# Last stage of a fused H3 and gated-MLP backward pass: partner spectra by a lane shuffle, halo rows by a shifted-identity matmul, merged weight-gradient stores, and a new order

## The chip, the cores and the metric

One core of one Trainium2 chip. The metric is device time in microseconds of one execution; a kernel's time is the median of several executions. The core has the engines TensorE (PE, with its weight loads PEld), VectorE (DVE), ScalarE (ACT), GpSimd (POOL) and SyncE (SP), and 16 DMA engines that all DMA queues share. In this kernel SP issues nearly all DMAs, and ACT issues some.

## The reference, cut to what matters

The reference computes the output of a block and, through `jax.vjp`, the gradients of nine inputs, for one sequence of S = 2048 tokens, D = 512 channels and F = 1376 hidden channels, in bf16:

```python
k_shift = sum over t of k_pad[:, t:t+S] * shift_k[:, 3-t]      # 4 taps per channel
kv = k_shift * v
y  = irfft(rfft(kv padded to 2S) * rfft(ssm_k padded to 2S))[:S] + kv * ssm_D
s  = xn * y                                                    # xn = layernorm(x)
h  = sigmoid(xn @ w_gate) * (xn @ w_up)
out = x + s * silu(h @ w_down)
# returned: out, and the gradients of x (A_q), k, v, shift_k, ssm_k, ssm_D, w_gate, w_up, w_down
```

The last stage, which the change edits, makes two groups of gradients. The weight gradients are products over all tokens: `d w_down = h^T dz` (1376 x 512) and `d w_gate`, `d w_up = xn^T dg`, `xn^T du` (512 x 1376 each). The gradients of k, v, shift_k, ssm_k and ssm_D go back through the long convolution: the spectrum of the incoming gradient is multiplied by the stored spectra of the kernel and of kv, and both products are transformed back.

## The kernel before, in words

Everything lives in one SBUF slab and one PSUM tile of 8 banks, and one helper (line 507) emits every instruction, so the profile puts almost all work on line 507 and calls its operands `slab` and `psum`. The code first records the operations of several streams (Python generators), and then a table of numbers, `ORDER`, gives for each engine the sequence in which the recorded operations are emitted; `moves` gives the common sequence of all DMAs, and `BANKS` gives each PSUM tile its banks. Every engine works through its own list in order: an instruction that waits holds up all that stand behind it on its engine, a DMA issue on ACT or SP too. Where an evacuation of PSUM may run on ACT or on DVE (`nc.evac`, line 413), the table decides.

Tokens are held as [128 partitions, 16, channels], token = 16 p + j. The channels are worked in 4 groups of 128 (`cg`). A transform of one group is `step1` (128x128 matmuls against a table of cosines and sines), `flip` (a DVE transpose of 32x32 blocks of 32-bit words, two halves q per group) and `step2` (lines 919 to 926): 16 matmuls of 32x32 by 32x512 that run side by side in the array, and two evacuations of [128, 1024].

The last stage runs three streams at once:

- `dW` (line 1285): 18 jobs, three weight gradients in 6 column blocks of up to 256. A job loads its transposed operand `L` by two DMA transposes on SP (`ld_L`, a ring of 3), does 64 matmuls (some 256 columns each), evacuates them on ACT in two halves into a ring of five [128, 512] buffers `ot`, and stores each half by a DMA that **ACT** issues. The load for job n+3 follows job n.
- `frontC` (line 1349): for each half transform n = 2 cg + q, `step2(Qt, Xc[:, 0])` makes the spectrum of the gradient, and `step2(Qt, Xc[:, 1], 5)` makes it a second time with real and imaginary rows swapped, from another 32x32 table (number 5, whose column pairs are those of table 0 exchanged).
- `backC` (line 1367): four DVE products of `Xc` with the stored spectra KK and VV, two inverse transforms (`inv2`: 32 small matmuls each, 2 evacuations and a DVE transpose; then `inv1`), the gradients of k and v (`dks`, and the lag loop of lines 1427 to 1441 on DVE), and the gradient of the taps (64 matmuls of 128x32, here called `pa`). `dks` needs 3 halo columns that belong to the next partition; two small SBUF-to-SBUF DMAs on SP bring them (lines 1398 and 1399).

`last_rows` (line 1443) makes the two small outputs of the taps and of ssm_D from the last group.

Of the kernel before, what the change touches and what calls it, by code (L numbers as in the profile page):

```python
# [11 lines left out]
f32 = mybir.dt.float32  # L12
# [4 lines left out]
P = 128  # L17
# [4 lines left out]
F = 1376  # L22
# [54 lines left out]
    """,  # L77
    "vector": """
# [44 lines left out]
    """,  # L123
    "gpsimd": """
        56+1 29+1 91 87 63 38 34 98 118 99+1 86 89+1 101 88 117 103 92 104 102 105+1 108 144 111 81 107 110 109 112
        229 503 119 937 914 1328 1659 1931 2263 3543 4847
    """,
    "sync": """
# [1401 lines left out]
```

## Time and profile before

| what | us |
|---|---|
| median of 3 runs (lowest, highest) | 450.49 (448.95, 450.92) |
| span of the profiled execution, first to last instruction | 447.7 |
| PE busy in it | 435.3 (97%) |
| DVE busy | 407.1 (91%) |
| ACT busy (DMA issues not counted) | 286.6 (64%) |
| granted PE clock, mean | 0.998 |

The profile page gives no other time for the profiled execution than its span; the median lies 2.8 us above the span, and this part lies outside the first and last instruction. A matmul is listed with its whole passage through the array, so consecutive ones overlap, and a busy PE is read from the distance of their starts. ACTq and SPq mark the issuing of DMAs or a wait in the queue of ACT or SP. DMA shares above 1 mean that packets wait for one another in the DMA engines.

### The profile page before, as it was taken

Reading aid. Unit: us, or ns where it says so; the run is one execution under the profiler, and the core shown is the slowest. Engines: PE = TensorE matmul, PEld = TensorE weight load, DVE = VectorE, ACT = ScalarE, POOL = GpSimd, SP = SyncE. Lnnn points to the kernel's source line nnn. Section 1 sums busy time; section 2 is a strip of 40 time slices with the busy share of each in tenths; the row PEclk is TensorE's granted clock in tenths of the full one; section 3 lists DMA queues with packets and bytes.
Section 4 is the critical chain, followed back from the end, with each engine's and each line's share of the span. In section 5 each row is a group of like instructions: output and inputs, shape, how many; then the busy total and the mean of one; then the engine's idle time right before and its main releaser. Section 6 shows DMA issues by size and latency. Waiting matters only on the chain.

```text
span 447.7 us, 11823 instructions
## 1 busy us (share of the span) xinstructions
PE 435.3 (97%) x4994; PEld 304.1 (68%) x5031; DVE 407.1 (91%) x621; ACT 286.6 (64%) x356; POOL 22.7 (5%) x48
## 2 busy tenths in 40 slices
PE   8999999999999999999999999999999999899995
PEld 3886686677768677655656655444577887777885
DVE  8999999999988699999999887789799899899993
ACT  7988788898758758685624523356557855366612
POOL 8202000011000000000000000000000000000000
PEclk9999999999999999999999999999999999999999
DMA  8999998798376999998999999999999999999998
GB/s 262 288 367 245 274 329 316 242 277 288 131 242 201 247 204 274 301 302 234 305 318 284 291 273 234 340 230 244 206 240 153 278 282 239 245 201 307 242 271 267
DMA packets 196702, 117.25 MB, mean 262 GB/s; under 512 B 107510, under 2 KB 183338, under 8 KB 196522
## 3 DMA queue, kind: packets, MB, share of 16 engines
q1 hardware_dynamic: 187496, 111.88, 96.3%
q10 hardware_dynamic: 9154, 4.62, 3.9%
q8 instruction: 39, 0.64, 0.6%
q14 instruction: 13, 0.11, 0.1%
HBM read 43.87 MB, written 46.70 MB: 202 GB/s over the span
## 4 chain that ended last, share of the span: by engine, by line
PE 87%; DMA 5%; DVE 3%; ACT 2%; issue 1%; ACTq 1%; POOL 0%; SPq 0%; DVEq 0%
PE psum L507 87%; DVE slab L507 3%; DMA slab<-duD 2%; ACT slab L507 2%; DMA out_dram<-slab 2%; DMA slab<-in_A_ssm_k_dram 1%; ACTq L507 1%; POOL slab L507 0%; SPq L507 0%; DVEq L507 0%
## 5 line engine op out<-in xcount | busy, mean ns | idle before, releaser
L507 PE MATMUL psum<-slab 128*128 128x256 bf16 (+5 forms) x4994 | 435.3, 301 | 7.9 <-ACT slab L507 2.5
L507 PEld LDWEIGHTS <-slab 128*128 128x128 bf16 (+3 forms) x5031 | 304.1, 96 | 138.9 <-issue 36.4
L507 ACT CAST slab<-psum 128x1024 bf16<-128x1024 f32 (+4 forms) x230 | 199.2, 908 | 130.3 <-PE psum L507 103.2
L507 DVE TENSOR_TENSOR slab<-slab 128x1024 bf16<-128x1024 bf16 (+4 forms) x302 | 240.2, 832 | 11.5 <-ACT slab L507 7.3
L507 DVE STREAM_TRANSPOSE slab<-slab 128x1024 f32<-128x1024 f32 x48 | 64.6, 1355 | 5.0 <-ACT slab L507 3.5
L507 ACT ACTIVATE slab<-slab 128x512 bf16<-128x512 bf16 (+5 forms) x61 | 51.5, 878 | 17.2 <-DVE slab L507 17.0
L507 DVE CAST slab<-psum 128x1024 bf16<-128x1024 f32 (+3 forms) x35 | 39.0, 1128 | 9.5 <-PE psum L507 7.2
L507 DVE TENSOR_TENSOR slab<-psum,slab 128x512 bf16<-128x512 f32 (+2 forms) x52 | 31.6, 607 | 2.7 <-PE psum L507 1.5
L507 ACT ACTIVATE slab<-psum 128x512 bf16<-128x512 f32 (+1 forms) x48 | 27.1, 571 | 5.0 <-PE psum L507 4.8
L507 POOL MEMSET slab<- 128x128 bf16 (+3 forms) x10 | 4.4, 437 | 276.6 <-DVE slab L507 139.5
L507 POOL TENSOR_TENSOR slab<-slab 128x2 f32<-128x2 f32 (+3 forms) x11 | 11.9, 1089 | 78.7 <-DVE slab L507 78.7
L507 DVE SCALAR_TENSOR_TENSOR slab<-slab 128x2 f32<-128x2 f32 (+2 forms) x41 | 14.7, 362 | 1.0 <-POOL slab L507 0.6
L507 ACT ACT_TABLE_LOAD x10 | 12.8, 1283 | 1.9 <-PEq L1514 1.7
L507 DVE SCALAR_TENSOR_TENSOR slab<-psum,slab 128x512 bf16<-128x512 f32 x16 | 10.9, 685 | 2.1 <-PE psum L507 2.1
L507 DVE BATCH_NORM_STATS2 slab<-slab 128x6 f32<-128x512 bf16 x16 | 10.6, 678 | 0.2 <-DMA slab<-in_A_q_dram 0.2
L507 DVE TENSOR_SCALAR slab<-slab 128x512 bf16<-128x512 bf16 (+6 forms) x28 | 7.4, 282 | 0.2
L507 ACT COPY slab<-psum 128x1024 bf16<-128x1024 bf16 (+2 forms) x7 | 5.3, 771 | 2.7 <-PE psum L507 2.7
L507 DVE COPY slab<-psum 128x512 bf16<-128x512 bf16 (+1 forms) x12 | 6.1, 527 | 0.9 <-PE psum L507 0.9
L507 POOL TENSOR_SCALAR slab<-slab 128x1 f32<-128x1 f32 (+3 forms) x10 | 3.4, 346 | 0.3
L507 DVE MEMSET slab<- 32x192 uint32 (+3 forms) x10 | 1.6, 160 | 1.3 <-PEq L1514 0.9
L507 DVE BATCH_NORM_AGGREGATE slab<-slab 128x2 f32<-128x6 f32 x16 | 2.5, 169 | 0.1
L507 POOL IOTA slab<- 128x32 f32 (+3 forms) x8 | 1.9, 320 | 0.4 <-POOLq L1514 0.4
(12 smaller groups left out, 7.5 us busy)
## 6 DMA issues: line engine op xcount, KB each, us to landing
slab<-KD SPq DMA_DIRECT2D x16, 512.0 KB, 5.2
hD<-slab SPq DMA_DIRECT2D x8, 704.0 KB, 6.1
duD<-slab SPq DMA_DIRECT2D x8, 704.0 KB, 7.8
dgD<-slab SPq DMA_DIRECT2D x8, 704.0 KB, 6.5
slab<-in_A_k_dram SPq DMA_DIRECT2D x4, 1024.0 KB, 8.6
KD<-slab SPq DMA_DIRECT2D x8, 512.0 KB, 6.0
VD<-slab SPq DMA_DIRECT2D x8, 512.0 KB, 2.8
out_dram<-slab SPq DMA_DIRECT2D x16, 256.0 KB, 5.2
```

What stands on the lines that cost most here:

```text
L507: getattr(getattr(self.nc, eng), meth)(*[place(v) for v in a], **{x: place(v) for x, v in k.items()})
```

## The change

What it does, part by part:

1. `frontC`: the second `step2` of each half transform goes. A DVE `stream_shuffle` of [128, 1024] 32-bit words exchanges neighbouring partitions (r with r^1 inside each block of 32) of `Xc[:, 0]` and writes `Xc[:, 1]`.
2. `backC`: the two halo DMAs per group go. A matmul with the identity shifted by one column ([128, 127] by [128, 384]) puts partition p+1 into row p of PSUM, and an evacuation of [127, 384] writes the halo.
3. `dW`: a job's two halves go to one `ot` buffer of [128, 1024] (a ring of 3 in place of five of [128, 512]) and to one store, issued by SP in place of ACT; only the last job keeps two stores.
4. `row4` and `row6` share a spectrum buffer in place of buffers of their own, and the mark that lets `frontC` be recorded further stands behind the second inverse transform.
5. `ORDER` and `BANKS` are new for the whole program, also for the first 270 us, whose operations are the same as before.

```diff
-    L_r, Xc_r, QV_r, QtV_r, ot_r = ar.rings((Ring, [NJ, 256], 3), (Ring, [2, 2048], 2), (WRing, 2048, 1), (WRing, 1024, 1), (Ring, [512], 5),
+    L_r, Xc_r, QV_r, QtV_r, ot_r = ar.rings((Ring, [NJ, 256], 3), (WRing, 2048, 2), (WRing, 2048, 1), (WRing, 1024, 1), (Ring, [1024], 3),
...
             elif s == 0:
-                for b in range(-(-w // 128)):
-                    kf = min(128, w - 128 * b)
+                ot = ot_r.next().rearrange("p (b d) -> p b d", b=2)
+                for b in range(2):
                     acc = ps("w", [512])
...
-                    ot = ot_r.next()
-                    nc.scalar.copy(ot[0:kf, :], acc[0:kf, :])
-                    nc.scalar.dma_start(out_9[f0 + b * 128:f0 + b * 128 + kf, :], ot[0:kf, :])
+                    nc.scalar.copy(ot[:, b], acc[:])
                     yield 16 * 512
+                nc.sync.dma_start(out_9[f0:f0 + 256, :].rearrange("(b p) d -> p b d", p=P), ot)
             else:
                 out = (out_7, out_8)[s - 1]
+                ot = ot_r.next().rearrange("p (b f) -> p b f", b=4)
...
-                    ot = ot_r.next().rearrange("p (b f) -> p b f", b=2)
-                    nc.scalar.copy(ot[:, :, 0:w], acc[:, :, 0:w])
-                    nc.scalar.dma_start(out[d2 * 256:(d2 + 1) * 256, f0:f0 + w].rearrange("(b p) f -> p b f", p=P), ot[:, :, 0:w])
+                    nc.scalar.copy(ot[:, 2 * d2:2 * d2 + 2, 0:w], acc[:, :, 0:w])
+                    if n == len(jobs) - 1:
+                        nc.sync.dma_start(out[d2 * 256:(d2 + 1) * 256, f0:f0 + w].rearrange("(b p) f -> p b f", p=P), ot[:, 2 * d2:2 * d2 + 2, 0:w])
+                if n < len(jobs) - 1:
+                    nc.sync.dma_start(out[:, f0:f0 + w].rearrange("(b p) f -> p b f", p=P), ot[:, :, 0:w])
...
-                Xc = stC["X", 2 * cg + q] = Xc_r.next()
+                Xc, Xw = Xc_r.next()
+                Xc = stC["X", 2 * cg + q] = Xc.rearrange("p (c n) -> p c n", c=2)
                 step2(Qt, Xc[:, 0])
-                step2(Qt, Xc[:, 1], 5)
-                yield 4096
+                nc.vector.stream_shuffle(Xw[:, 1024:2048], Xw[:, 0:1024], [r ^ 1 for r in range(32)])
+                yield 2048
...
-            nc.sync.dma_start(dks[0:112, NJ:NJ + 3, :], dks[1:113, 0:3, :])
-            nc.sync.dma_start(dks[112:127, NJ:NJ + 3, :], dks[113:128, 0:3, :])
+            ph = ps("x", [3 * GW])
+            nc.tensor.matmul(ph[0:127, :], ident[:, 1:P], dks[:, 0:3, :].rearrange("p j d -> p (j d)"), start=True, stop=True)
+            nc.evac(dks[0:127, NJ:NJ + 3, :].rearrange("p j d -> p (j d)"), ph[0:127, :], 384)
```

How the new table moves instructions, at three places.

**ACT, the middle of the last stage (stores of jobs 8 to 10 of dW).** A `CAST slab<-psum` is an evacuation, `DMA out_dram<-slab` a weight-gradient store. Before:

```order
236 L507 CAST slab<-psum 128x1024
237 L507 DMA out_dram<-slab 128x2x256
238 L507 CAST slab<-psum 128x1024 x2
239 L507 CAST slab<-psum 128x128x8
240 L507 DMA out_dram<-slab 128x2x256 x2
241 L507 CAST slab<-psum 128x1024
242 L507 CAST slab<-psum 128x512
243 L507 DMA out_dram<-slab 128x2x256
```

Now, at the same part of the stage:

```order
219 L524 CAST slab<-psum 128x512
220 L524 CAST slab<-psum 128x1024
221 L524 CAST slab<-psum 128x512
222 L524 CAST slab<-psum 128x1024
223 L524 CAST slab<-psum 128x128x8
224 L524 CAST slab<-psum 128x1024 x2
225 L524 CAST slab<-psum 128x512
226 L524 CAST slab<-psum 128x1024
```

All 35 stores have left ACT's list for the rest of the stage; on SP stand 19 merged ones.

**DVE, the first half transforms of frontC.** `STREAM_TRANSPOSE 128x1024` is a flip, the CASTs of 128x1024 are evacuations, the products of 128x2048 belong to backC. Before:

```order
357 L507 STREAM_TRANSPOSE slab<-slab 128x1024
358 L507 TENSOR_TENSOR slab<-slab 128x2048
359 L507 STREAM_TRANSPOSE slab<-slab 128x32x16x2
360 L507 CAST slab<-psum 128x1024 x3
361 L507 STREAM_TRANSPOSE slab<-slab 128x1024
```

Now:

```order
330 L524 CAST slab<-psum 128x1024
331 L524 STREAM_TRANSPOSE slab<-slab 128x1024
332 L524 STREAM_SHUFFLE slab<-slab 128x1024
333 L524 CAST slab<-psum 128x1024 x2
334 L524 TENSOR_TENSOR slab<-slab 128x2048 x3
335 L524 TENSOR_TENSOR slab<-slab 128x512
336 L524 TENSOR_TENSOR slab<-slab 128x2048
337 L524 STREAM_SHUFFLE slab<-slab 128x1024
```

Over the whole program the CASTs of 1024 columns from PSUM go from 30 to 23 on DVE and from 170 to 161 on ACT; eight shuffles come to DVE.

**SP, the end of the program.** Before, the last DMAs of SP were these (ACT issued the last weight-gradient stores beside them):

```order
226 L507 DMA out_dram<-slab 2048x1x256
227 L507 DMA out_dram<-slab 128x8x256
228 L507 DMA out_dram<-slab 128x2048
229 L507 DMA out_dram<-slab 128x8x256
230 L507 DMA out_dram<-slab 4x512
231 L507 DMA out_dram<-slab 4x128
```

Now:

```order
237 L524 DMA out_dram<-slab 128x8x256
238 L524 DMA out_dram<-slab 2048x1x256
239 L524 DMA out_dram<-slab 128x8x256
240 L524 DMA out_dram<-slab 128x2x96
241 L524 DMA out_dram<-slab 128x4x256
242 L524 DMA out_dram<-slab 4x128
243 L524 DMA out_dram<-slab 128x4x256
244 L524 DMA out_dram<-slab 128x2x96
245 L524 DMA out_dram<-slab 128x2048
246 L524 DMA out_dram<-slab 4x512
```

The store of 128x2048 (512 KB, the ssm_k gradient of the last group) has moved from the fourth-last place to the second-last, behind the weight-gradient stores, and the row of 4x512, which needs the last DVE copies, is now the last DMA of all.

More of the change, by code (lines that the diff above doesn't have):

```diff
@@ L33 @@
     "tensor": """
[43 rows of a table removed]
[62 rows of a table added]
     """,
     "vector": """
[25 rows of a table removed]
[25 rows of a table added]
     """,
     "scalar": """
[17 rows of a table removed]
[15 rows of a table added]
     """,
     "gpsimd": """
-        56+1 29+1 91 87 63 38 34 98 118 99+1 86 89+1 101 88 117 103 92 104 102 105+1 108 144 111 81 107 110 109 112
-        229 503 119 937 914 1328 1659 1931 2263 3543 4847
+        56+1 29 87 30 63 92 88 38 34 89 98 91 86 99 90 117 100+1 118 103+2 107+1 106 109 81 110 144 102 119 111+1 229
+        503 937 914 1328 1659 1931 2263 3543 4774
     """,
     "sync": """
[11 rows of a table removed]
[11 rows of a table added]
     """,
     "moves": """
[12 rows of a table removed]
[12 rows of a table added]
     """,
@@ L156 @@
 BANKS = (
-    "22302000232103101001321110100010000101130100101000011101011001001001223011100001100001013101011002011011001011"
-    "00001111101021010101010100100101010011000110101001101001100111032101101012333101211012301030100301000110123001"
-    "01010100021210201201321020211031232112222110202320212301223012122102032012002203110231002131210210202122030210"
-    "01203311103012103100101102210301313"
+    "33300311012220003001211110100010000101120000101000011101011001031001032011100001100001013101011002011011001011"
+    "00001111100021010101010100100101010001000110101001101000101101032102101012310101321003101032101231010110023001"
+    "01011100021210100101020211003211232011020220221302321121202210211012013222223331021223102102122301120231010301"
+    "21031001012102330301321"
 )
@@ L1266, in kernel_impl @@
             (Ring, [2048], 2), (Ring, [2048], 2), (Ring, [2048], 2), (WRing, 1024, 1), (Ring, [NJ, GW], 1), (Ring, [128, NJ], 1),
-            (Ring, [NJ, GW], 1), (Ring, [512], 1), (Ring, [256], 1), (Ring, [GW], 1))
-    L_r, Xc_r, QV_r, QtV_r, ot_r = ar.rings((Ring, [NJ, 256], 3), (Ring, [2, 2048], 2), (WRing, 2048, 1), (WRing, 1024, 1), (Ring, [512], 5),
+            (Ring, [NJ, GW], 1), (Ring, [256], 1))
+    L_r, Xc_r, QV_r, QtV_r, ot_r = ar.rings((Ring, [NJ, 256], 3), (WRing, 2048, 2), (WRing, 2048, 1), (WRing, 1024, 1), (Ring, [1024], 3),
                                             freed=[b for r in dead for b in r.blks], then=late)
@@ L1299, in dW @@
                     nc.tensor.transpose(pt[0:96, db, :], ot[:, db * 96:(db + 1) * 96], ident)
-                ot = ot_r.next()
+                ot = ot[:, 512:1024]
                 nc.scalar.copy(ot[0:96, :], pt[0:96].rearrange("p a k -> p (a k)"))
-                nc.scalar.dma_start(out_9[f0:F, :], ot[0:96, :])
+                nc.sync.dma_start(out_9[f0:F, :], ot[0:96, :])
                 yield 512
             elif s == 0:
-                for b in range(-(-w // 128)):
-                    kf = min(128, w - 128 * b)
+                ot = ot_r.next().rearrange("p (b d) -> p b d", b=2)
+                for b in range(2):
                     acc = ps("w", [512])
                     for j in range(NJ):
-                        nc.tensor.matmul(acc[0:kf, :], L[:, j, b * 128:b * 128 + kf], dzA[:, j, :], start=(j == 0), stop=(j == NJ - 1))
-                    ot = ot_r.next()
-                    nc.scalar.copy(ot[0:kf, :], acc[0:kf, :])
-                    nc.scalar.dma_start(out_9[f0 + b * 128:f0 + b * 128 + kf, :], ot[0:kf, :])
+                        nc.tensor.matmul(acc[:], L[:, j, b * 128:b * 128 + 128], dzA[:, j, :], start=(j == 0), stop=(j == NJ - 1))
+                    nc.scalar.copy(ot[:, b], acc[:])
                     yield 16 * 512
+                nc.sync.dma_start(out_9[f0:f0 + 256, :].rearrange("(b p) d -> p b d", p=P), ot)
             else:
                 out = (out_7, out_8)[s - 1]
+                ot = ot_r.next().rearrange("p (b f) -> p b f", b=4)
                 for d2 in range(2):
@@ L1385, in backC @@
                     nc.vector.tensor_tensor(Xc[:, i], Xc[:, i], VV, ALU.mult)
-                stC["nY"] = n + 1
                 inv2([(Y, 3), (KK, 4)], q, B1w)
@@ L1389, in backC @@
                 inv2([(Xc[:, 0], 3), (Xc[:, 1], 4)], q, B2w, 1)
+                stC["nY"] = n + 1
                 ld_KV(n + 2)
@@ L1443, in last_rows @@
     def last_rows():
+        row4, row6 = (v[:, a:b] for v, a, b in zip(2 * [VV_r.next()], (0, 512), (512, 640)))
         for lag in range(4):
@@ L1462, in kernel_impl @@
         r.free()
-    kh_r, vg_r, B1_r, B2_r, dks_r, KK_r, VV_r, Y_r, Bq_r, ksh_r, dKT_r, term_r, row4_r, dm_r, row6_r = ar.rings(
+    kh_r, vg_r, B1_r, B2_r, dks_r, KK_r, VV_r, Y_r, Bq_r, ksh_r, dKT_r, term_r, dm_r = ar.rings(
         *late)
-    row4, row6, dm = row4_r.ap, row6_r.ap, ar.view(dm_r.blks[0][0], [4, 32], f32)
+    dm = ar.view(dm_r.blks[0][0], [4, 32], f32)
     ld_KV(0)
```

233 rows, old and new, of the table ORDER are left out of this document.

## The prediction, made before the result was known

> **What bounds the kernel now.** I read the page's busy shares first, then the waits of PE, the chain of waits, and PE and DVE by stretches of the last stage.
>
> ```profile
> PE 435.3 (97%) x4994; PEld 304.1 (68%) x5031; DVE 407.1 (91%) x621; ACT 286.6 (64%) x356; POOL 22.7 (5%) x48
> ...
> PE psum L507 <- ACT slab L507: 2.5, 2, 1.8
> PE psum L507 <- DVE slab L507: 1.8, 2, 1.3
> PE psum L507 <- issue: 1.1, 7, 0.2
> PE psum L507 <- DMA slab<-in_A_ssm_k_dram: 0.7, 1, 0.7
> ```
>
> In the second part (line: engine <- releaser: us in total, times, longest) PE waits for all others together some 6 us of a span of 447.7. So PE bounds the kernel, and the time moves by what PE no longer does, by the few waits it has, and by what lies behind its last matmul. The stretches of the last stage (us; busy PE, PEld, DVE, ACT, POOL; clock; DMA share; GB/s) show how much cover the others have:
>
> ```profile
> 360.00:380.00 20.00, 20.00 (x358) 16.82 (x340) 19.35 (x21) 11.98 (x14) 0.73 (x1) 1.00 1.16 282
> 380.00:400.00 20.00, 18.18 (x299) 15.33 (x297) 18.10 (x18) 10.51 (x14) 0.00 (x0) 1.00 1.13 231
> 400.00:410.00 10.00, 10.00 (x162) 7.49 (x160) 9.13 (x9) 6.51 (x8) 0.00 (x0) 1.00 1.14 264
> 410.00:420.00 10.00, 10.00 (x148) 7.83 (x146) 9.96 (x9) 6.76 (x8) 0.00 (x0) 1.00 1.15 241
> ```
>
> PE is full except in one stretch; DVE is at 90 to 100% and the DMA engines always have packets waiting (share above 1). The clock is 1.00, so nothing is to be had there. The hole in 380 to 400 is one event, seen in ACT's timeline (start, length, ACTq is the issuing of DMAs) and in the chain of waits (start, length, what):
>
> ```profile
> 380.25 1.01 ACT L507 CAST slab<-psum 128x1024 bf16<-128x1024 f32 x1 [0.34 <-PE psum L507]
> 380.31 4.56 ACTq L507 DMA_DIRECT2D out_dram<-slab  x2
> 384.91 1.50 ACT L507 CAST slab<-psum 128x1024 bf16<-128x1024 f32 x2 [3.65 <-DMA out_dram<-slab]
> ...
> 375.44 9.02 DMA slab<-duD
> 384.47 0.02 issue
> 384.49 0.38 ACTq L507
> 384.87 0.04 issue
> 384.91 1.02 ACT slab L507
> ...
> 382.79 1.36 PE L507 MATMUL psum<-slab 128*128 128x256 bf16 x11
> 385.97 1.22 PE L507 MATMUL psum<-slab 128*128 128x96 bf16 x25 [1.82 <-ACT slab L507]
> ```
>
> ACT's second store could not be issued before a DMA transpose of SP, issued at 375.44, had landed at 384.47. Behind it stood an evacuation that PE needed: ACT lost 3.65 us, PE 1.82. The other wait of PE for ACT (2.5 in all, so 0.7) has the same look at 308: two stores in 1.61 us, and the next evacuation late.
>
> ```profile
> 307.99 1.61 ACTq L507 DMA_DIRECT2D out_dram<-slab  x2
> 309.69 1.50 ACT L507 CAST slab<-psum 128x512 bf16<-128x512 f32 x2 [1.74 <-PE psum L507]
> ```
>
> **The change part by part.** The sum is made against the span of 447.7; the median is 2.8 above it, and I add the sum to the median.
>
> *Second `step2`, 8 times 16 matmuls.* Weight loads show what a block of small matmuls costs:
>
> ```profile
> 397.14 0.14 PEld L507 LDWEIGHTS <-slab 32*32 32x32 bf16 x16 [0.21 <-issue]
> 397.51 0.33 PEld L507 LDWEIGHTS <-slab 128*128 128x128 bf16 x4 [0.23 <-issue]
> ...
> 370.43 0.77 PEld L507 LDWEIGHTS <-slab 32*32 32x32 bf16 x48 [0.21 <-issue]
> 371.43 0.66 PEld L507 LDWEIGHTS <-slab 128*128 128x128 bf16 x7 [0.23 <-issue]
> ```
>
> A block of 16 takes 397.51 - 397.14 = 0.37 us to the next large weights, one of 48 takes 1.00: (1.00 - 0.37) / 2 = 0.32 for each further 16, which holds some waiting; 512 columns at the pace of the 11 matmuls above ((1.36 - 0.27) / 10 = 0.109 us for 256 columns, 0.27 the passage of the last) are 0.22. I take 0.26: 8 x 0.26 = **-2.1** (bounds -1.7 and -2.6).
>
> *Entering and leaving the small mode.* Each visit also costs the two idle stretches in the rows, 0.21 + 0.23 = 0.44. Counted in the order of the whole program, visits fall from 55 to 52 (-1.3), but the 64 `pa` matmuls of two groups are now cut up between small ones, 6 more changes inside visits, at 0.37 - 0.22 = 0.15 each (+0.9): **-0.4** (bounds -1.3 and +1.3, the latter if an inner change costs 0.44 too). The Trainium skill (TensorEngine Tiling, Tiling Modes) says that every change of tiling mode drains TensorE. By that rule the removal of half the `step2` calls saves no visit by itself; the rows agree, since 16 matmuls fewer in a block leave the 0.44 as it was, and with an inner change as dear as a full one this term would be +1.3.
>
> *Halo matmul.* 4 matmuls of 384 columns: 4 x 384/256 x 0.109 = **+0.65**. Their weights load under the matmul before, as all large ones do. No DVE or PE work waits for the removed DMAs in a row of the waits, so their removal is worth nothing on the path; it takes 8 issues from SP.
>
> *ACT and DVE.*
>
> ```profile
> L507 ACT CAST slab<-psum 128x1024 bf16<-128x1024 f32 x170 | 166.9, 1016 | 79.2 <-PE psum L507 60.5 <-DVE slab L507 10.6 <-DMA out_dram<-slab 6.2
> L507 DVE TENSOR_TENSOR slab<-slab 128x2048 bf16<-128x2048 bf16 x109 | 130.1, 1211 | 3.0 <-issue 1.7 <-DMA slab<-KD 0.8
> L507 DVE STREAM_TRANSPOSE slab<-slab 128x1024 f32<-128x1024 f32 x48 | 64.6, 1355 | 5.0 <-ACT slab L507 3.5 <-PE psum L507 1.2
> L507 DVE CAST slab<-psum 128x1024 bf16<-128x1024 f32 x30 | 36.1, 1216 | 8.1 <-PE psum L507 5.8 <-ACT slab L507 1.8 <-issue 0.5
> ```
>
> 16 evacuations go: 9 from ACT (9 x 1.02 = 9.2 us) and 7 from DVE (7 x 1.22 = 8.5). No shuffle is in the trace. The nearest rows move the same 1024 words: the product of 2048 bf16 at 1.21 below, the transpose at 1.36 above; if it went by bf16 elements at a word's pace, 2 x 1.21 = 2.4. The transpose is nearest (32-bit words across partitions), so 8 x 1.36 = 10.9, and DVE gets +2.4 us (from +1.2 to +10.7). The Trainium skill (VectorE: DVE Perf Modes, The perf-mode tier table) gives a shuffle about 2400 ns for 2048 elements, at one element a cycle; as an estimate that is 1.2 us here and DVE +1.1; no run here shows it. Over the last 140 us DVE idles some 6%, about 8 us, so +2.4 is hidden under PE, and +10.7 would not be. Three of the four halo evacuations go to ACT, which has just lost nine longer ones. On PE's path: **0**.
>
> *Stores to SP.* ACT's queue holds no DMA in the last stage any more, so neither of its two waits can come back there: **-2.5** (bounds 0, if the evacuations are late for another reason, and -2.5). SP gets 19 stores, loses 8 halo DMAs, and works in order:
>
> ```profile
> out_dram<-slab ACTq DMA_DIRECT2D x30, 128.0 KB, 5.4
> ...
> slab<-duD SPq DMA_TRANSPOSE x12, 5.6
> ```
>
> A store behind an evacuation holds up the next transposes. Between the last use of a ring slot and the first use of its next load, the new order has at least 9.1 us of matmul columns, counted at 0.109 for 256 (6.9 before; 9.5 to 11 for the other late jobs before, 11 to 13 now), against 5.6 for a landing. I allow one new wait of the size of the smaller old one, rounded up: **+0.9**.
>
> *The end.* ACT's last evacuation and store, and the stretches after:
>
> ```profile
> 443.40 0.32 ACT L507 CAST slab<-psum 128x192 bf16<-128x192 f32 x1 [1.28 <-PE psum L507]
> 443.75 0.38 ACTq L507 DMA_DIRECT2D out_dram<-slab  x1
> ...
> 443.00:444.00 1.00, 0.13 (x4) 0.00 (x0) 0.00 (x0) 0.32 (x1) 0.00 (x0) 1.00 1.14 348
> 444.00:445.00 1.00, 0.00 (x0) 0.00 (x0) 0.00 (x0) 0.00 (x0) 0.00 (x0) 1.00 1.17 303
> 445.00:446.00 1.00, 0.00 (x0) 0.00 (x0) 0.00 (x0) 0.00 (x0) 0.00 (x0) 1.00 0.15 35
> ```
>
> PE ends at 443.1, the DMA engines empty at 445.1, the span ends 4.6 after PE. Now 512 KB are issued second-last, about 0.8 us behind PE's end; at 348 GB/s they need 1.5 us, so the engines empty at about PE + 2.3 to 3 in place of + 2.0: **+0.5** (bounds 0 and +1.5).
>
> *The head.* The K load stood behind an issue of `A_shift_k` of 0.42 us and PE waited 0.7 for it; now it is the second DMA of SP: **-0.4** (0 to -0.7).
>
> Sum: -2.1 - 0.4 + 0.65 - 2.5 + 0.9 + 0.5 - 0.4 = -3.35. Time: 450.49 - 3.35 = **447.1 us**.
>
> **The rivals.**
>
> *The waits for ACT only change place.* PE stays without the -2.5 and keeps the rest: 450.49 - 0.85 = 449.6. For it: the landing at 384.47 was late because the DMA engines were full, and they stay as full, with the same bytes. Against it: the landing held ACT only through a store in its list. The Trainium skill (DMA: Bandwidth & Descriptors, Issuing engines are not separate DMA queues) speaks for it: all DMAs share 16 engines, and the issuer only saves its own issue time. By that rule alone the move is worth what ACT idles anyway; the row of 3.65 us disagrees, as the saved issue time is a whole landing.
>
> *SP becomes the bound: slower.* A merged store waits on SP for its second evacuation and for older landings, and the transposes behind it go late. It decides as soon as the delay eats the 9.1 - 5.6 = 3.5 us of slack. If PE then waits 0.5 us in each of the 15 jobs whose load follows a store, that is 7.5 in place of 0.9: 447.1 + 6.6 = 453.7. For it: every landing takes 5 to 9 us and the DMA share is above 1. Against: the wider windows, and fewer DMAs in all.
>
> *The end grows.* DVE's last copies now feed PE's last four matmuls and the last DMA, and 512 KB lie before it. With +2.4 us DVE ends behind the weight gradients and the tail grows by 1.5 more: 448.6.
>
> *The shuffle takes 2.4 us.* DVE's 8 us of idle time are gone and 2.7 us show: 449.8. Only a small chance, since the flip of as many words takes 1.36.
>
> **How the numbers follow.** Chances: forecast 0.50, ACT's waits move 0.24, longer end 0.08, dear shuffle 0.04, SP bound 0.14. Of the forecast's cases all but 0.02 lie below 448.2, and some of the longer end (0.02) too. What this kernel's measurements can tell from no change is about 0.5%, 2.25 us: below 448.24 is faster, above 452.74 slower. Faster 0.50, same 0.37, slower 0.13. The forecast's own range, from the bounds of its terms, is 445.0 to 449.0; the range that holds 8 in 10 reaches to the rivals above, 444.6 to 451.9.
>
> **What would show it.** In the profile after: PE's busy time some 2 us lower; no row of ACT waiting for a DMA `out_dram`, and PE's wait for ACT under 1 us; a DVE row STREAM_SHUFFLE x8 at 1.2 to 1.4 us; blocks of 16 small weight loads where 32 stood. It is wrong if PE shows waits for DMA `duD` or `dgD` (SP bound), if DVE in 400 to 440 is full and PE waits for it, or if more than 5.5 us lie behind PE's last large matmul.

## The result, and the profile after

| | before | after |
|---|---|---|
| median of 13 runs (lowest, highest), us | 449.30 (447.37, 451.48) | 446.46 (444.88, 447.89) |
| ratio, with its 95% interval | | 0.9935 (0.9913 to 0.9958) |
| span of the profiled execution | 447.7 | 444.3 |
| last matmul ends at | 443.1 | 438.2 |
| from there to the end of the span | 4.6 | 6.1 |

The change makes the kernel faster by 0.65% (0.42 to 0.87%), 2.9 us of 449.3. In the profiled executions it is 3.4 us; PE ends 5.0 us earlier, and 1.5 of that are lost behind it. In the executions of the changed kernel the time is 2.3 us above the span (446.62 against 444.3 in the profiled one); of the 2.8 us between the median and the span before, given above, some 0.5 are therefore the difference of two executions and do not lie outside the first and last instruction. The prediction's sum does not use this part.

The page of the changed kernel, busy time by engine, and its groups by form (mean ns of one behind the comma):

```profile
PE 433.5 (98%) x4871; PEld 303.7 (68%) x4907; DVE 409.9 (92%) x630; ACT 279.8 (63%) x351; POOL 21.8 (5%) x48
```

```profile
L524 ACT CAST slab<-psum 128x1024 bf16<-128x1024 f32 x161 | 158.7, 1016 | 86.4 <-PE psum L524 75.3 <-DVE slab L524 10.4 <-ACT slab L524 0.2
L524 DVE CAST slab<-psum 128x1024 bf16<-128x1024 f32 x23 | 27.9, 1217 | 3.7 <-PE psum L524 3.5
...
L524 DVE STREAM_SHUFFLE slab<-slab 128x1024 f32<-128x1024 f32 x8 | 10.6, 1320 | 0.0
```

The evacuations fell as counted, 9 on ACT and 7 on DVE; a shuffle takes 1.32 us, and DVE works 2.8 us longer. The waits of PE:

```profile
PE psum L524 <- DVE slab L524: 1.9, 2, 1.3
PE psum L524 <- issue: 0.8, 5, 0.2
```

Of the old rows, PE's waits for ACT (2.5) and for the load of `ssm_k` (0.7) are gone, and no new one stands in their place. The stretch of 380 to 400, where PE had its hole, is full, and so is DVE (us; busy PE, PEld, DVE, ACT, POOL; clock; DMA share; GB/s). Behind PE's end at 438.2 the DMA engines run on until 441.2:

```profile
380.00:400.00 20.00, 20.00 (x297) 17.15 (x295) 19.76 (x22) 11.57 (x17) 0.00 (x0) 1.00 1.16 227
...
438.00:439.00 1.00, 0.16 (x2) 0.00 (x0) 0.00 (x0) 0.57 (x1) 0.00 (x0) 1.00 1.11 330
...
440.00:441.00 1.00, 0.00 (x0) 0.00 (x0) 0.00 (x0) 0.00 (x0) 0.00 (x0) 1.00 0.90 344
441.00:442.00 1.00, 0.00 (x0) 0.00 (x0) 0.00 (x0) 0.00 (x0) 0.00 (x0) 0.62 0.26 92
```

The prediction did not ask how full SP itself is. Its rows in the timeline of the changed kernel (start, length in us, operation):

```profile
402.93 3.93 SPq L524 DMA_TRANSPOSE slab<-duD  x1
406.95 0.54 SPq L524 DMA_DIRECT2D out_dram<-slab  x1
407.54 0.58 SPq L524 DMA_DIRECT2D slab<-in_A_k_dram  x1
408.21 6.41 SPq L524 DMA_TRANSPOSE slab<-duD  x1
414.68 0.58 SPq L524 DMA_DIRECT2D out_dram<-slab  x1
415.35 2.73 SPq L524 DMA_TRANSPOSE slab<-duD  x1
418.13 0.63 SPq L524 DMA_DIRECT2D out_dram<-slab  x1
418.86 4.19 SPq L524 DMA_TRANSPOSE slab<-duD  x1
423.14 4.67 SPq L524 DMA_DIRECT2D out_dram<-slab  x3
427.90 1.86 SPq L524 DMA_TRANSPOSE slab<-duD  x1
429.86 1.63 SPq L524 DMA_DIRECT2D out_dram<-slab  x2
```

From 402.93 to 431.49 they add up to 27.75 of 28.56 us (a row of several holds the gaps between them, here some 1.8 us). A plain DMA keeps SP for 0.5 to 0.6 us, and the row of a transpose is 1.9 to 6.4 us long. How much of such a row is work of SP and how much is waiting stays open. The view of SP's waits from 402 to 432 puts 13.9 us down to PE:

```profile
SPq L524 <- PE psum L524: 13.9, 4, 5.6
```

These are the four transposes issued at 402.93, 408.21, 415.35 and 427.90. Counting the 64 matmuls of each job in the trace, the ring slots that they write had been read for the last time 2 us or more before (at 395.8, 406.0, 406.0 and 415.8), so it was not the slot that they waited for. But the rows are no fixed price either, as two runs below show. So PE and DVE are full in this stage, and SP's list shows next to no gap. The runs ask which of them the time follows.

### The profile page after: what moved, and what is told of

Same layout as the page of the kernel before. It is cut to its first block, busy times and chain, and to the rows that moved or that the text cites. A ratio compares the mean times of both kernels' runs of the same rounds, so it can differ in the third digit from the quotient of the medians.

```text
span 444.3 us, 11521 instructions
## 1 busy us (share of the span) xinstructions
PE 433.5 (98%) x4871; PEld 303.7 (68%) x4907; DVE 409.9 (92%) x630; ACT 279.8 (63%) x351; POOL 21.8 (5%) x48
## 4 chain that ended last, share of the span: by engine, by line
PE 94%; DVE 2%; issue 1%; DMA 1%; POOL 0%; ACT 0%; DVEq 0%
PE psum L524 94%; DVE slab L524 2%; DMA slab<-in_A_q_dram 1%; POOL slab L524 0%; ACT slab L524 0%; DVEq L524 0%
## 5 line engine op out<-in xcount | busy, mean ns | idle before, releaser
L524 PEld LDWEIGHTS <-slab 128*128 128x128 bf16 (+2 forms) x4907 | 303.7, 96 | 134.2 <-issue 30.1
L524 ACT CAST slab<-psum 128x1024 bf16<-128x1024 f32 (+3 forms) x224 | 192.0, 897 | 128.6 <-PE psum L524 112.7
L524 ACT ACTIVATE slab<-slab 128x512 bf16<-128x512 bf16 (+5 forms) x59 | 49.5, 879 | 23.9 <-DVE slab L524 23.7
L524 DVE CAST slab<-psum 128x1024 bf16<-128x1024 f32 (+3 forms) x29 | 31.4, 1089 | 5.6 <-PE psum L524 5.2
L524 DVE STREAM_SHUFFLE slab<-slab 128x1024 f32<-128x1024 f32 x8 | 10.6, 1320 | 0.0
L524 ACT COPY slab<-psum 128x512 bf16<-128x512 bf16 (+2 forms) x10 | 7.4, 755 | 2.6 <-PE psum L524 2.6
L524 DVE TENSOR_SCALAR slab<-slab 128x512 bf16<-128x512 bf16 (+6 forms) x30 | 8.4, 299 | 0.1
L524 DVE COPY slab<-psum 128x512 bf16<-128x512 bf16 (+1 forms) x9 | 4.6, 526 | 0.2 <-PE psum L524 0.2
```

The source lines that it names most:

```text
L524: getattr(getattr(self.nc, eng), meth)(*[place(v) for v in a], **{x: place(v) for x, v in k.items()})
```

## The experiments

All were timed beside the kernel before. "Against the changed kernel" is the difference of two ratios, times 449 us; the half-widths of the two intervals (0.22% and about 0.25%) combine, as the root of their squares, to about 1.5 us either way (1.7 for the halo by DMA). The runs on the changed kernel keep its order, which was made for its own edits; no new order was made for any of them, so part of each difference may be a worse fit of the order.

| kernel | median, us | ratio to before (95%) | against the changed kernel, us |
|---|---|---|---|
| the changed kernel | 446.46 | 0.9935 (0.9913 to 0.9958) | |
| before, stores on SP only | 454.47 | 1.0114 (1.0076 to 1.0152) | (+5.1 against before) |
| before, shuffle only | 449.07 | 1.0004 (0.9982 to 1.0026) | (+0.2 against before) |
| before's order, all edits | 462.34 | 1.0302 (1.0275 to 1.0328) | (+13.6 against before) |
| changed, halo by DMA | 450.45 | 1.0021 (0.9991 to 1.0051) | +3.9 |
| changed, stores split in two | 450.80 | 1.0020 (0.9992 to 1.0048) | +3.8 |
| changed, stores on ACT | 447.75 | 0.9968 (0.9942 to 0.9994) | +1.5 |
| changed, small matmuls twice | 447.69 | 0.9973 (0.9952 to 0.9993) | +1.7 |
| changed, 32 large matmuls less | 446.63 | 0.9948 (0.9924 to 0.9973) | +0.6 |
| changed, 16-bit shuffle | 450.81 | 1.0053 (1.0033 to 1.0073) | +5.3 |
| changed, 480 KB less stored | 446.14 | 0.9931 (0.9906 to 0.9957) | -0.2 |
| changed, early store | 445.88 | 0.9932 (0.9906 to 0.9958) | -0.1 |
| changed, end on two queues | 447.02 | 0.9959 (0.9937 to 0.9980) | +1.1 |

### Before, with only the stores on SP

```diff
-                    nc.scalar.dma_start(out_9[...], ot[0:kf, :])      # and the two other stores of dW
+                    nc.sync.dma_start(out_9[...], ot[0:kf, :])
```

> The kernel before with its order, where only the 35 weight-gradient stores are issued by SP in place of ACT, unmerged and at their old place among the DMAs. Theory P (PE's waits set the time, as predicted): both waits of PE for ACT go, -2.5 us. Rival M (the waits only move place): PE's sum of waits stays, within 0.5 us of before. Rival D (the DMA engines are full to the end and empty behind PE's last matmul, so the backlog of transfers sets the end): PE ends some 2 us earlier, but the span falls by less than 1 us and the tail behind PE grows by the difference. Rival S (SP becomes the bound): slower, PE waits for DMA dgD or duD.

Measured: +5.1 us against before, not -2.5. Its waits of PE, then rows of its timeline, two rows of its chain of waits, and a stretch with the clock:

```profile
PE psum L512 <- ACT slab L512: 3.2, 4, 1.8
PE psum L512 <- DVE slab L512: 3.1, 3, 1.3
PE psum L512 <- DMA slab<-duD: 1.1, 1, 1.1
```

```profile
354.60 1.23 DVE L512 TENSOR_TENSOR slab<-slab 128x2048 bf16<-128x2048 bf16 x1 [3.46 <-DMA slab<-KD]
...
364.50 7.96 PE L512 MATMUL psum<-slab 128*128 128x128 bf16 x122 [1.30 <-DVE slab L512]
...
373.63 1.50 ACT L512 CAST slab<-psum 128x512 bf16<-128x512 f32 x2 [2.87 <-DMA out_dram<-slab]
...
374.27 19.92 PE L512 MATMUL psum<-slab 128*128 128x256 bf16 x329 [1.81 <-ACT slab L512]
```

```profile
345.70 8.81 DMA slab<-KD
...
366.87 6.66 DMA out_dram<-slab
```

```profile
374.00:376.00 2.00, 1.73 (x9) 1.20 (x9) 1.21 (x2) 1.13 (x2) 0.00 (x0) 0.57 0.45 104
376.00:378.00 2.00, 2.00 (x13) 1.44 (x12) 2.00 (x3) 0.00 (x0) 0.00 (x0) 0.58 0.83 215
```

The two old waits at 308 and 380 are gone. But DVE waits 3.46 us for a load of a stored spectrum (`KD`), and PE for DVE some time later. This load was not issued late: SP issued it at 345.70, and in the kernel before at 346.13:

```profile
346.13 0.38 SPq L507 DMA_DIRECT2D slab<-KD  x1
```

It landed late, at 354.5 in place of 352.5. PE's longest wait is again one for ACT behind a store, by another way than before: ACT's evacuation waits 2.87 us for a store issued by SP at 366.87 to land at 373.53, and PE 1.81 for ACT. The prediction's "neither of its two waits can come back there" held for ACT's queue, not for what ACT's instructions themselves wait for. Behind the gap of 1.81 us the granted clock is 0.50 from 374.3 to 377.7; by the matmuls lost in 3.4 us at half the clock that costs some 1.7 us more, as an estimate.

So the run is slower, as rival S said, but only one of its waits, the 1.1 for `duD`, is of the kind that S named. Rival D does not show as it was put, since PE itself ends later (448.8). Landings that take longer on full DMA engines are not excluded: whether the stores cost their places in SP's list or the transfers beside them stays open in this run.

### Before, with only the shuffle

```diff
-    L_r, Xc_r, QV_r, QtV_r, ot_r = ar.rings(..., (Ring, [2, 2048], 2), ...
+    L_r, Xc_r, QV_r, QtV_r, ot_r = ar.rings(..., (WRing, 2048, 2), ...
...
-                step2(Qt, Xc[:, 1], 5)
+                nc.vector.stream_shuffle(Xw[:, 1024:2048], Xw[:, 0:1024], [r ^ 1 for r in range(32)])
```

> The kernel before with its order, where only the second step2 of each visit (16 small matmuls and two evacuations) is a stream shuffle on DVE. P: PE loses 8 x 0.26 = 2.1 us of matmuls, visits to the small mode go by what stands between; -1.5 to -2.5 us. Rival (DVE is full and PE waits for it): DVE gets +2 us of work in an order not made for it, gain under 0.5 us with new PE waits for DVE. D: PE ends about 2 us earlier, the span falls by less than 1.

Measured: 1.0004, no gain from 128 small matmuls less.

```profile
PE psum L510 <- DVE slab L510: 3.5, 4, 1.5
PE psum L510 <- ACT slab L510: 2.5, 5, 1.2
```

```profile
360.00:380.00 20.00, 18.51 (x315) 15.85 (x314) 19.70 (x23) 7.97 (x10) 0.73 (x1) 1.00 1.02 237
```

DVE is full (19.70 of 20), and PE's waits for it went from 1.8 to 3.5 us; PE's waits for ACT are 2.5 in sum as before, now five of up to 1.2. The rival named in the expectation holds: the interval, -0.8 to +1.2 us, leaves out the -1.5 to -2.5 of P.

### The halo by DMA again

```diff
-            ph = ps("x", [3 * GW])
-            nc.tensor.matmul(ph[0:127, :], ident[:, 1:P], ...)
-            nc.evac(dks[0:127, NJ:NJ + 3, :]..., ph[0:127, :], 384)
+            nc.sync.dma_start(dks[0:112, NJ:NJ + 3, :], dks[1:113, 0:3, :])
+            nc.sync.dma_start(dks[112:127, NJ:NJ + 3, :], dks[113:128, 0:3, :])
```

> The changed kernel with the halo copied by two DMAs from slab to slab in each of the four groups again, in place of the matmul and its evacuation. P (as predicted: the matmul costs 0.65 us on PE, the removal of the DMAs is worth nothing): -0.65 us against the changed kernel. D (the 0.39 MB in small packets lie on full DMA engines): PE ends 0.65 us earlier or at the same time, but the engines empty 1 to 2 us later: +1 to +2 us against the changed kernel.

The DMAs stand in SP's list where their data were ready in the trace of the changed kernel. Measured: +3.9 us against the changed kernel. Its waits of PE, its timeline, and two stretches:

```profile
PE psum L528 <- DMA slab<-duD: 3.6, 2, 2.3
```

```profile
423.77 11.56 PE L528 MATMUL psum<-slab 128*128 128x256 bf16 x183 [1.22 <-DMA slab<-duD]
...
425.56 1.54 SPq L528 DMA_DIRECT2D slab<-slab  x2
427.20 4.03 SPq L528 DMA_DIRECT2D out_dram<-slab  x3
431.31 1.66 SPq L528 DMA_TRANSPOSE slab<-duD  x1
...
437.67 6.05 PE L528 MATMUL psum<-slab 128*128 128x96 bf16 x67 [2.34 <-DMA slab<-duD]
```

```profile
439.00:440.00 1.00, 1.00 (x7) 0.67 (x7) 0.36 (x2) 0.74 (x2) 0.00 (x0) 0.54 1.15 348
440.00:441.00 1.00, 1.00 (x6) 0.75 (x5) 0.00 (x0) 0.00 (x0) 0.00 (x0) 0.50 1.15 348
```

The last transpose is issued at 431.31, in the changed kernel at 427.90, and PE waits for it. The size is above what D gave, and the way is another: PE itself ends at 443.7 in place of 438.2. Of these 5.5 us the waits for `duD` are 3.6, and the clock, 0.50 from 439.1 to 442.5, makes some 1.7 by estimate. At these places of SP's list, eight more DMAs cost more than the matmuls that replace them.

### The merged stores split

```diff
-                nc.sync.dma_start(out_9[f0:f0 + 256, :]..., ot)
+                for b in range(2):
+                    nc.sync.dma_start(out_9[f0 + 128 * b:f0 + 128 * b + 128, :], ot[:, b])
...
-                    nc.sync.dma_start(out[:, f0:f0 + w]..., ot[:, :, 0:w])
+                    for d2 in range(2):
+                        nc.sync.dma_start(out[d2 * 256:(d2 + 1) * 256, f0:f0 + w]..., ot[:, 2 * d2:2 * d2 + 2, 0:w])
```

> The changed kernel, where each of its 16 merged stores is two stores again, one right behind the other on SP at the place of the merged one: the same bytes, the same order, 16 more DMAs on SP. S (places in SP's queue are the scarce thing): loads come later, PE waits for DMA dgD or duD, or for DVE that waits for a load; +2 to +4 us against the changed kernel, about as much as the 8 halo DMAs cost. B (bytes and order count, not the number): within 0.5 us of the changed kernel.

```profile
PE psum L530 <- DMA slab<-duD: 3.0, 2, 1.5
```

Measured: +3.8 us, as S said, with the wait it named. The bytes and the order are the same; 16 more places in SP's list at 0.5 to 0.6 us are some 9 us of SP. SP does not fall behind by as much: with 25 in place of 18 other DMAs between them, the last twelve transposes keep SP for 38.7 us in place of 43.7. The last one is issued at 432.63, 4.7 us later.

### The merged stores on ACT

```diff
-                nc.sync.dma_start(out_9[f0:f0 + 256, :]..., ot)       # and the other stores of dW
+                nc.scalar.dma_start(out_9[f0:f0 + 256, :]..., ot)
```

> The changed kernel, where the 19 merged weight-gradient stores are issued by ACT again, each right behind its last evacuation; SP keeps everything else in its order. P (as predicted: a store on ACT costs PE the waits for late evacuations): ACT rows wait for DMAs again, PE waits for ACT 2 us or more, +2 to +3 us against the changed kernel. S (SP's queue is the scarce one: it issues for 17 to 19 of every 20 us of the last stage): SP gets air, loads come earlier, PE's waits for ACT come back but the sum is within 1 us of the changed kernel.

```profile
PE psum L529 <- ACT slab L529: 1.3, 2, 0.7
```

Measured: +1.5 us (0.0 to 3.0). PE's waits for ACT come back, two of 0.6 to 0.7, smaller than before; no DMA that ACT would wait for is named in its rows. The value lies between P and S, at the edge of what can be told from nothing. SP got no air, other than S had it: with 11 in place of 18 other DMAs between them, the last twelve transposes keep SP for 47.0 us in place of 43.7, and the last one is issued at 427.06 (427.90 in the changed kernel). Transposes of the same size thus take less of SP when more stands between them and more when less does. What stretches them, the full DMA engines behind SP or something else, no run here separates.

### More and less work on PE

```diff
-    def step2(Qt, dst, t=0):
+    def step2(Qt, dst, t=0, n=1):
...
-        for r in range(4):
+        for r in [0, 1] * n + [2, 3] * n:
...
-                step2(Qt, Xc[:, 0])
+                step2(Qt, Xc[:, 0], 0, 2)        # in frontC: each matmul twice
```

> The changed kernel, where the 16 small matmuls of each of the 8 step2 blocks are issued twice (the second time they write the same values again; nothing is evacuated twice). It measures the disputed cost of 16 small matmuls by itself. P: 8 x 0.26 = +2.1 us against the changed kernel, PE's busy time +2.1. D or S: +0.5 to +1.2 us, since the DMA engines catch up meanwhile.

```profile
440.00:442.00 2.00, 0.39 (x4) 0.09 (x1) 0.00 (x0) 0.79 (x2) 0.00 (x0) 1.00 0.97 290
```

PE is busy until 440.39 in place of 438.16: 2.2 us for 8 x 16 small matmuls, 0.28 each block, beside 0.26 in the sum. These are the ends of one execution each. Counted in the trace of the changed kernel, a block of 16 mostly takes 0.37 us from its first matmul to the next large one and a block of 32 takes 0.58, so a second 16 take 0.22. The time follows by 1.7 us (0.3 to 3.1); this holds P's 2.1 and the 0.5 to 1.2 of the rivals alike.

```diff
-                        for j in range(NJ):
+                        nj = 8 if (s, u) == (2, 0) else NJ
+                        for j in range(nj):
...
-                                             start=(j == 0), stop=(j == NJ - 1))
+                                             start=(j == 0), stop=(j == nj - 1))
```

> The changed kernel, where one of the 18 weight-gradient jobs (the first of out_8, about 395 to 400) adds up 8 of its 16 terms, so that 32 matmuls of 256 columns are left out and that part of out_8 is half a sum. P: 32 x 0.109 = 3.5 us less on PE, -3.0 to -3.5 us against the changed kernel. D or S (the DMA engines or SP's queue are as full as PE): PE waits for DMA duD later on or the tail grows; -0.5 to -1.5 us.

```profile
PE psum L529 <- ACT slab L529: 2.2, 4, 0.9
PE psum L529 <- DVE slab L529: 1.8, 2, 1.3
PE psum L529 <- DMA slab<-duD: 1.7, 2, 1.1
```

3.5 us less on PE (this job runs from 385 to 396 in the changed kernel) bring nothing measurable (+0.6, -0.9 to +2.1): PE reaches its operands before they are there and waits 3.9 us more for ACT and for transposes. The profiled execution took 448.8 us, 2.2 above the median of this kernel, so a middling one will wait less. So the changed kernel is about balanced: more work on PE costs, less gains nothing that can be told.

### A shuffle that takes longer

```diff
-                nc.vector.stream_shuffle(Xw[:, 1024:2048], Xw[:, 0:1024], [r ^ 1 for r in range(32)])
+                nc.vector.stream_shuffle(Xc[:, 1], Xc[:, 0], [r ^ 1 for r in range(32)])     # bf16 views
```

> The changed kernel, where each of the 8 shuffles moves 2048 bf16 elements in place of 1024 32-bit words, the same bytes. If the price goes by elements, it takes 2 x 1.32 = 2.6 us, DVE's busy time grows by 10 us, DVE's idle time in the last stage (about 6 us of 160) is gone and PE waits for DVE: +2 to +4 us against the changed kernel. If it goes by bytes: 1.3 us and no change.

```profile
L524 DVE STREAM_SHUFFLE slab<-slab 128x2048 bf16<-128x2048 bf16 x8 | 18.3, 2293 | 0.0
```

```profile
PE psum L524 <- DVE slab L524: 3.6, 7, 1.3
PE psum L524 <- ACT slab L524: 2.0, 3, 1.0
```

The price goes by elements, 2.29 against 1.32 us. DVE's 7.7 us more (18.3 against 10.6) cost 5.3 us (3.8 to 6.8), above the 2 to 4 expected: DVE's cover was thinner than its 6 to 8 idle microseconds.

### All edits in the old order

The changed code with the tables of before: what stays keeps its place; a shuffle stands where DVE came to it in the trace of before, a halo matmul where its data were ready, a merged store at the place of the second of its two.

> All edits of the change (shuffle, halo matmul, merged stores on SP) in the order of the kernel before: instructions that stay keep their places, each shuffle stands where DVE came to it in the trace of before, each halo matmul where its data were ready, each merged store at the place of the second of its two. P (the terms of the sum belong to the edits): -3 to -4 us against before, like the changed kernel. O (the new order is what turns the edits into time): PE waits of 3 us or more for DVE, ACT or loads, and -2 to +2 us against before.

```profile
PE psum L508 <- DVE slab L508: 7.8, 8, 3.0
PE psum L508 <- ACT slab L508: 5.0, 1, 5.0
```

```profile
DVE slab L508 <- DMA out_dram<-slab: 6.2, 1, 6.2
```

```profile
318.00:322.00 4.00, 2.48 (x28) 0.70 (x28) 3.91 (x4) 3.43 (x4) 0.00 (x0) 0.50 0.90 223
322.00:326.00 4.00, 4.00 (x36) 1.38 (x35) 1.33 (x2) 1.11 (x2) 0.00 (x0) 0.71 0.00 0
```

Measured: +13.6 us against before, worse than both theories. One event makes much of it: at 310 DVE waits 6.2 us for a store before it may write a buffer, ACT waits for DVE and PE 5.0 us for ACT, and the clock is halved afterwards. Buffers lie at the changed kernel's addresses here, so this run mixes the missing order with the places of the buffers. It shows that these edits do not gain without an order made for them, and not what the order alone is worth: the old operations in a new order were not run.

### The end

Three runs looked at the 1.5 us by which the end grew between the two profiled executions. In the first, the last 512 KB store stands before the last four weight-gradient stores (a change of the tables only). In the second, three of these four are issued by ACT as well. In the third, an earlier store is cut:

```diff
+            w = 128 if cg == 2 else 2048
-            nc.sync.dma_start(out_5[c0:c1, :], dKT...)
+            nc.sync.dma_start(out_5[c0:c1, 0:w], dKT...[:, 0:w])
```

> The changed kernel, where the 512 KB store of the last out_5 is issued before the last four weight-gradient stores in place of behind them (its data are ready at 434.6, it was issued at 438.77). Theory T (the tail grew because this store is issued late): the span behind PE's end falls from 6.1 to about 5.1, -0.8 to -1.0 us against the changed kernel. Rival D (the same bytes have to go through full DMA engines, whatever their order): engines empty at 3 us behind PE as now, within 0.3 us of the changed kernel.

> The changed kernel with a shorter end: the last out_5 store before the last weight-gradient stores as in the early-store run, and three of these last four stores on ACT, which has nothing else to do between its last evacuations, so that two queues issue the last transfers. T (the end is set by when the last stores are issued): the span behind PE's end falls from 6.1 to 4.0 to 4.8 us, -1.3 to -2 us against the changed kernel, and at most 0.5 better than the early-store run. Rival (the DMA engines are full there anyway): the tail stays at 5.5 to 6, no gain.

> The changed kernel, where the store of out_5 for the third group (512 KB, issued at 414.7, 30 us before the end) writes 32 KB only, so that most of these rows of out_5 are left out. P (PE sets the end): within 0.3 us of the changed kernel. D (the DMA engines set the end): they empty up to 480 KB / 345 GB/s = 1.4 us earlier, and the span falls by 0.8 to 1.4 us with PE's end unmoved.

None of them moved the time measurably: -0.1, +1.1 and -0.2 us, each 1.4 to 1.5 either way. That leaves out T's -1.3 to -2 for two queues; it does not leave out the -0.8 to -1.0 of the early store, nor the -0.8 to -1.4 of fewer bytes. The profile of the early store looks like a success, span 442.5 and 4.6 us behind PE's end; but the 13 executions of the changed kernel have spans of 442.6 to 445.6, and the second run, with the same early store, has 6.6 us behind PE's end (438.9 to 445.6). In the other runs on the changed kernel, whose last DMAs are largely the same, 4.4 to 6.7 us lie behind PE's end. One profile cannot tell a microsecond at the end, and so the growth by 1.5 us is not established either.

## Why the prediction was right, and where it was not

The forecast, 447.1 us, is 0.6 above the median, and -3.35 us stands beside -2.9 measured (-3.4 in the profiles). The sum started from 450.49, the median of the three executions known then, 1.2 us above the median of 13 (449.30); from there the same sum would have given 446.0, 0.5 below. Of its signs, PE's busy time (1.8 us lower), the rows of ACT, the shuffle's row and the blocks of 16 came as named, and no wait of PE for `duD` or `dgD` came. One sign of being wrong came too: more than 5.5 us, 6.1, lie behind PE's last matmul, and so behind its last large one. By its own steps:

- **What bounds.** "PE bounds" is half of it. PE's work costs time when it is added (2.2 us of PE, 1.7 of time), and is worth nothing when it is taken away, in the changed kernel (3.5 us, nothing) as in the one before (shuffle only, nothing). The second is not a clean test, since the shuffle loads DVE as it unloads PE. DVE is as full as PE, and SP's list has next to no gap. The prediction saw DVE's 90 to 100% and the DMA shares, and took them for cover.
- **Second `step2`, -2.1.** The price is right: 0.22 to 0.28 against 0.26 for 16. That it becomes time hangs on the order, since alone it brought nothing.
- **Small mode, -0.4, and halo matmul, +0.65.** Neither was measured by itself; the traces have the 55 and 52 visits that were counted. The removal of the halo DMAs, "worth nothing on the path", is the first step that failed: putting them back into the changed kernel costs 3.9 us. The prediction looked for somebody who waits for a halo; the ones who wait stand behind it on SP. The old order held the same eight DMAs without a wait of PE for `duD`, so this is their price in the new order.
- **ACT and DVE, 0.** The shuffle at 1.36 was 1.32, and DVE's +2.4 was +2.8. Hidden in the new order, not in the old. The rival of a dear shuffle, 2.7 us for one of 2.4 us, had the right shape and half the size: with 2.29 it cost 5.3.
- **Stores to SP, -2.5, bounds 0 and -2.5.** The second step that failed. Both waits of PE for ACT went, as it said. But 35 stores on SP without the rest cost 5.1 us, outside the bounds. The bounds asked only about ACT's queue. In that run ACT waited for stores all the same, 2.87 us at 373.63, and DVE for a load that landed late; the sum had no term for either. In the new order and merged, the stores on SP are worth 1.5 (0.0 to 3.0). The Trainium skill (DMA: Bandwidth & Descriptors, Issuing engines are not separate DMA queues) says that issuing DMAs on several engines at once only saves the sequencer's time to initiate them, which is usually small beside the DMA. In these runs the choice of the issuer was not small: +5.1 us in the old order.
- **One new wait, +0.9.** It did not come. This term alone is most of the 1.15 us by which PE ended earlier than summed. The split stores and the halo DMAs show that 8 to 16 more DMAs on SP would have brought it, with 3.0 to 3.6 us and not 0.9. So "SP becomes the bound", held for 0.14, is the true neighbour of this change: 453.7 was said, and 450.5 to 454.5 is what kernels with more DMAs on SP take.
- **The end, +0.5, bounds 0 and +1.5.** In the two profiles it is +1.5, at the bound. Its reason, the 512 KB issued second-last, is neither borne out nor excluded: moving that store changes the time by -0.1 us, 1.5 either way. The engines empty 3.9 us earlier than before (441.2 against 445.1) and PE ends 5.0 earlier. What holds them back stays open; cutting 480 KB 30 us before the end does not help measurably.
- **The head, -0.4.** The wait of 0.7 for `ssm_k` is gone from the rows; it was not tested alone.

So the sum is right in part by luck, since two terms were off in opposite directions: PE ended 5.0 us earlier where the terms ahead of the end gave 3.85, and the end took 1.0 more, each read from one execution before and one after. And the terms do not belong to the edits: alone in the old order, the stores cost 5.1 us and the shuffle brings nothing, and all edits together cost 13.6. Of the kernels run, only those with the edits and the order made for them gain. The likely way is that SP's list stays just short enough (8 halo DMAs less, 16 stores saved by merging: +3.9 and +3.8 us when put back) while SP takes over the stores that held up ACT. How much of the 2.9 us the new order would bring without the edits is not shown. None of the kernels run beats the changed one measurably.

## What to carry to other kernels

Before moving a DMA from one queue to another, look at the queue that gets it, in the stage where it goes: how long its list has no gap, which loads stand behind the new place, and who waits for them. Adding up the rows of a queue does not tell how much room it has, since the transposes here took 38.7 to 47.0 us of the same list by what stood between them; test it. Look also at who waits for the moved DMA to land, not only at the queue in which it stood. Where PE, DVE and a DMA queue all show next to no gap, the price of an edit is not a property of the edit: test it in the order that it will run in, and do not count on a cut in one of them before the others have air too. A transfer for which no one waits is not free while loads queue behind it.

## What was unexpected of the hardware

A gap in PE can cost more than its length. At the end of 1.81 us without work the granted clock fell to 0.50 for 3.4 us (374.3 to 377.7, stores on SP only); 1.4 us after a gap of 2.34 us it fell to 0.50 for 3.4 us (439.1 to 442.5, halo by DMA); within a gap of 5.0 us it fell to 0.50 for 6.8 us (317.5 to 324.3, old order). The wait of 1.82 us in the kernel before left it at 1.00. The Trainium skill (TensorE: Matmul & The Clock Gate, What's actually happening) has the clock halved after an idle window of about 3.4 us that runs free of the kernel's start; the halving and its length agree, but here a gap of about half a window was enough at one place and not at another.

The shuffle's price goes by elements and not by bytes: (2293 - 1320) / 1024 = 0.95 ns for each element of a partition beyond 1024. The Trainium skill (VectorE: DVE Perf Modes, The perf-mode tier table) gives about 2400 ns for 2048 elements; 2293 for bf16 is 4% below.
